# A gated linear attention followed by a routed expert layer: work reordered in the attention stage, tables turned, banks kept

## The chip, the cores and the metric

The kernel runs on one core of one Trainium2 chip. Times are device microseconds (us) of that core, from one launch. Engines are called PE (matrix products, with PEld for its weight loads), DVE (vector), ACT (scalar), POOL (GpSimd) and SP (which only issues transfers here). Each engine executes its own instructions strictly in the order in which the program issues them.

## The reference

q, k, v and alpha have shape (4 batches, 8 heads, 768 rows, 48). Per batch and head a 48x48 state is kept:

```
state = alpha[t][:, None] * state + outer(k[t], v[t])
y[t]  = q[t] @ state
x     = y with the heads side by side, (3072, 384)
on    = x @ w_skip > 0                     # rows that are computed at all
e     = argmax(x @ w_gate)  (8 experts)    # gate = softmax value of e
out   = x + gate * (relu(x @ w1[e]) @ w2[e])   for rows that are on, else x
```

w1[e] is 384x1024 and w2[e] 1024x384. All is float32.

## The kernel before, in words

**Attention stage.** The 3072 rows are cut into 24 tiles of 128 rows, six per batch, the four batches in turn. Tile i arrives in one buffer `qkv` (alpha, k, q transposed, then v). DVE makes two scans along the rows, `suffix` (L212) and `prefix` (L222), whose results scale k and q (L228 and L232, nearly all on POOL). Step i of the loop in `attention` then issues on PE, in this order: `scores(i+1)` (L252, k times q), `inter(i)` (L289, the product of the old state with q, from tile 4 on), `turn_k(i+1)` (L273, up to tile 19), `rows(i-1)` (L336, the finished output turned back to rows, with the nine routing columns), `outer(i)` (L301, the state's update, up to tile 19) and `intra(i)` (L309, masked scores times v). `inter(i)` and `intra(i)` add into one accumulator `ps_y`, which ACT copies out in `take_y` (`xt`, L316); the next tile's `inter` writes the same tile of PSUM. ACT also copies scores (L258), keys (L275) and rows (L347); POOL masks the left half of the scores (L262), DVE the right half (L266) and updates the state (L328).

**Routing.** `route_group` handles tiles 0-7, 8-14 and 15-19 as groups, in small DVE instructions that the loop lets out a few per step (`tick`). It computes the chosen expert, the gate and the rank of each row within its expert; then for each tile a 128x256 one-hot matrix of the rank (`one_hot`; ACT in two instructions, L460 and L461, or DVE in one, L457), and `marks` (L470) multiplies it with the row numbers and gates to fill a table, slot by expert. The one-hot is the stationary operand, 128x128 twice. Tiles 20-23 go one by one through `route_one`. For expert 0 its rows from these late tiles are not fetched from memory but selected by a product with a one-hot (`late_rows`, L533), the others are fetched by an indirect transfer (`fetch_rows`, L560) and turned (`early_turn`); `first_turn` copies the sum out.

**Weights.** Every weight piece is split in a high and a low part: ACT casts (L589), DVE or POOL subtracts (L590). Expert 0's w1 and w2 are both split during attention, in 12 pieces of 512 columns on ACT and POOL; expert e+1's during expert e, w1 beside the `up` products and w2 beside the `down` products.

**Expert stage.** For each of 8 experts `up` issues 72 products (L648) in four groups g of 18, `turn` (L628) prepares the next expert's rows, `down` issues 48 products for each half (L663), and rows are scattered to memory (L668). Within expert 0, `finish_table` adds the last marks after `up(0, 0)`. The attention's PSUM pool is closed before, and new ones (`ps_x`, `ps_h`, `ps_o`, `ps_f`) are opened.

## Time and profile before

| | us |
|---|---|
| median of 3 runs | 301.01 |
| lowest and highest | 300.92, 301.5 |
| the profiled execution | 301.59 |
| its span, first to last instruction | 299.9 |

| engine | busy us | share of the span | instructions |
|---|---|---|---|
| PE | 278.0 | 93% | 2831 |
| DVE | 201.4 | 67% | 393 |
| ACT | 142.9 | 48% | 290 |
| POOL | 152.1 | 51% | 176 |

A share is a mean over stages with different limits. PE counts as busy at either clock: the granted TensorE clock is 1.00 at its full level (2.4 GHz) and 0.50 at the lower one (1.2 GHz), and its mean over this execution is 0.939.

### The profile page before, as it was taken

The numbers are of one execution on the slowest core, as the hardware profiler recorded it, in microseconds if no ns is written. First come the engines' busy times: TensorE is split into PE (matmuls) and PEld (weight loads), VectorE is DVE, ScalarE is ACT, GpSimd is POOL, SyncE is SP. The second block draws the span as 40 slices with busy tenths as digits, with TensorE's granted clock in tenths as the row PEclk, the third lists the DMA queues.
The fourth block names the chain that finished last, engine by engine and source line by source line (L and its number), as shares of the span: only waits on it lengthen the run. The fifth ranks groups of instructions, "written<-read, shape, count | busy, mean of one in ns | idle before, by whom it ended". The sixth has DMA issues, their size and how long they took to land.

```text
span 299.9 us, 7149 instructions
## 1 busy us (share of the span) xinstructions
PE 278.0 (93%) x2831; PEld 260.0 (87%) x2831; DVE 201.4 (67%) x393; ACT 142.9 (48%) x290; POOL 152.1 (51%) x176
## 2 busy tenths in 40 slices
PE   7799999998998899779499999999999999999991
PEld 7689888887887787668499999999999999999990
DVE  5889788986778667743637675776757686785410
ACT  4335544668855954332328165471726538173200
POOL 6579987798779887551127431505133150302111
PEclk9789999999799989756979999999999999999998
DMA  7998899898489964342004676564667645550000
GB/s 240 320 375 300 283 313 313 275 318 294 155 271 322 316 228 138 105 115 105 26 3 108 251 256 237 184 211 163 228 234 249 233 165 178 198 208 26 12 29 20
DMA packets 20201, 60.04 MB, mean 200 GB/s; under 512 B 3272, under 2 KB 7181, under 8 KB 20160
## 3 DMA queue, kind: packets, MB, share of 16 engines
q1 hardware_dynamic: 17984, 54.43, 53.5%
q0 software_dynamic: 2176, 5.08, 4.8%
q8 instruction: 24, 0.39, 0.5%
q14 instruction: 17, 0.14, 0.1%
HBM read 52.46 MB, written 8.65 MB: 204 GB/s over the span
## 4 chain that ended last, share of the span: by engine, by line
PE 82%; DVE 9%; ACT 4%; POOL 2%; issue 1%; DMA 1%; POOLq 0%; DVEq 0%
PE ps_h L648 23%; PE ps_o L663 22%; PE ps_s L252 8%; PE ps_y L309 6%; PE ps_g L336 6%; PE ps_y L289 4%; PE ps_v L301 3%; PE ps_k L273 3%; PE ps_v L470 2%; DVE sfx L212 2%; PE ps_x L628 2%; DVE pfx L222 2%; ACT far L460 1%; PE ps_k L336 1%; DMA qkv<-in_tiles_dram 1%
## 5 line engine op out<-in xcount | busy, mean ns | idle before, releaser
L668 POOL DMA_INDIRECT out_dram<-o,idx x16 | 22.5, 1408 | 92.2 <-DVE o L666 92.2
L648 PE MATMUL ps_h<-xx,w1h 128*128 128x256 f32 x384 | 59.6, 286 | 3.1 <-DVE all L457 3.1
L648 PEld LDWEIGHTS ps_h<-xx,w1h 128*128 128x128 f32 x384 | 52.6, 193 | 3.4 <-ACT idg L434 3.3
L652 ACT ACTIVATE hh<-ps_h 128x512 fp32r<-128x512 f32 x32 | 19.1, 598 | 70.5 <-PE ps_h L648 69.8
L663 PE MATMUL ps_o<-w2h,hh 128*128 128x384 f32 x128 | 43.6, 341 | 0.0
L663 PE MATMUL ps_o<-w2h,hl 128*128 128x384 f32 x128 | 43.0, 336 | 0.0
L663 PE MATMUL ps_o<-w2l,hh 128*128 128x384 f32 x128 | 43.0, 336 | 0.0
L653 DVE SCALAR_TENSOR_TENSOR hl<-ps_h,hh 128x512 fp32r<-128x512 f32 x32 | 22.1, 692 | 20.8 <-ACT hh L652 20.5
L648 PE MATMUL ps_h<-xx,w1l 128*128 128x256 f32 x192 | 34.4, 285 | 0.0
L228 POOL TENSOR_TENSOR qkv<-qkv,sfx 112x512 f32<-112x512 f32 x24 | 28.5, 1187 | 11.5 <-DVE sfx L212 9.2
L252 PE MATMUL ps_s<-qkv 48*128 48x128 f32 x384 | 30.6, 300 | 3.0 <-DVE qkv L232 2.8
L252 PEld LDWEIGHTS ps_s<-qkv 48*128 48x128 f32 x384 | 25.8, 201 | 8.0 <-issue 5.5
L212 DVE TENSOR_TENSOR_SCAN sfx<-qkv,ps_d 112x524 f32<-112x524 f32 x24 | 29.6, 1233 | 3.8 <-DMA qkv<-in_tiles_dram 3.8
L309 PE MATMUL ps_y<-st,qkv 128*48 128x128 f32 x384 | 31.8, 306 | 0.0
L666 DVE SCALAR_TENSOR_TENSOR o<-ps_o,gates,xr 128x384 f32<-128x384 f32 x16 | 9.9, 618 | 31.0 <-PE ps_o L663 31.0
L222 DVE TENSOR_TENSOR_SCAN pfx<-qkv,ps_d 112x524 f32<-112x524 f32 x24 | 29.6, 1235 | 0.2
L560 POOL DMA_INDIRECT xr<-out_dram,idx x18 | 22.0, 1225 | 13.4 <-DVE gates L618 5.6
L648 PEld LDWEIGHTS ps_h<-xx,w1l 128*128 128x128 f32 x192 | 28.2, 193 | 0.0
L232 POOL TENSOR_TENSOR qkv<-qkv,pfx 112x512 f32<-112x512 f32 x22 | 26.2, 1190 | 3.4 <-DVE pfx L222 3.3
L590 DVE TENSOR_TENSOR w1l<-raw,w1h 128x768 fp32r<-128x768 f32 x28 | 26.9, 960 | 0.8
L589 ACT CAST w1h<-raw 128x768 fp32r<-128x768 f32 (+1 forms) x34 | 26.8, 789 | 0.0
L309 PEld LDWEIGHTS ps_y<-st,qkv 128*48 128x48 f32 x384 | 24.9, 138 | 0.6 <-issue 0.4
(166 smaller groups left out, 518.9 us busy)
## 6 DMA issues: line engine op xcount, KB each, us to landing
raw<-in_w_dram SPq DMA_DIRECT2D x64, 384.0 KB, 4.8
qkv<-in_tiles_dram SPq DMA_DIRECT2D x21, 966.0 KB, 6.7
out_dram<-x SPq DMA_DIRECT2D x24, 192.0 KB, 6.0
qkv<-in_tiles_dram SPq DMA_DIRECT2D x3, 262.0 KB, 5.1
out_dram<-xr SPq DMA_DIRECT2D x4, 192.0 KB, 7.6
qkv<-in_tiles_dram SPq DMA_DIRECT2D x1, 704.0 KB, 4.3
qkv<-in_tiles_dram SPq DMA_DIRECT2D x2, 256.0 KB, 3.5
qkv<-in_tiles_dram SPq DMA_DIRECT2D x1, 512.0 KB, 5.4
```

The costliest lines, as they stand in the source:

```text
L212: nc.vector.tensor_tensor_scan(sfx[:PD][:, ::-1], w["alpha"][:PD][:, ::-1], self.c_r[:PD].to_broadcast([PD, AW]), LOW, ALU.mult, ALU.max)
L222: nc.vector.tensor_tensor_scan(pfx[:PD], w["alpha"][:PD], self.c_f[:PD].to_broadcast([PD, AW]), 0.0, ALU.mult, ALU.max)
L228: (eng or self.nc.gpsimd).tensor_tensor(w["kh"][:PD], w["kh"][:PD], w["sfx"][:PD, :, 3:SEG], ALU.mult)
L232: (eng or nc.gpsimd).tensor_tensor(w["qh"][:PD], w["qh"][:PD], w["pfx"][:PD, :, 2:2 + P], ALU.mult)
L252: nc.tensor.matmul(self.ps_s[h][:, p * P:(p + 1) * P], lhsT=kh[r, p, :], rhs=qh[r, p, :], start=True, stop=True)
L309: nc.tensor.matmul(self.y_out(i, p, h), lhsT=w["v"][:, o:o + D], rhs=w["st"][:, h, p * P:(p + 1) * P], start=(i < B and p < 2), stop=(p >= 2))
L589: nc.scalar.copy(out=hi[:, s], in_=raw[:, s])
L590: (nc.gpsimd if early else nc.vector).tensor_tensor(lo[:, s], raw[:, s], hi[:, s].bitcast(F32), ALU.subtract)
L648: nc.tensor.matmul(ps[:, u, :], lhsT=a[:, k, f * P:(f + 1) * P], rhs=xx[:, k, b, :], start=(n == 0), stop=(n == len(order) - 1))
L653: nc.vector.scalar_tensor_tensor(out=hl, in0=ps, scalar=0.0, in1=hh.bitcast(F32), op0=ALU.max, op1=ALU.subtract)
L663: nc.tensor.matmul(ps, lhsT=a[:, f, js], rhs=b[:, f, :], start=(n == 0), stop=(n == 3 * FT - 1))
L668: ins = nc.gpsimd.indirect_dma_start(out=self.out[:, :], out_offset=bass.IndirectOffsetOnAxis(ap=self.idx[:, e, j:j + 1], axis=0), in_=o, ...
```

## The change

- **Order.** In a step, `inter(i)` is issued after `rows(i-1)`, before `outer(i)`. For tile 0 `outer`, `intra` and `carry` stand before `scores(1)`.
- **Start.** Loads are cut and ordered anew; the first tile's scans go in halves, with products by halves on DVE and POOL. The zero fills of `xw`, `stb`, `xtb` move from POOL to DVE, those of the three row buffers to ACT (one per step 1 to 3), and `route_constants` from step 3 to the start. For tiles 0 and 1 the right half of the scores goes through ACT and POOL as the left does. There are 14 warm-up products, and 4 more behind `turn_k(0)`.
- **Routing.** Groups are tiles 0-5, 6-10, 11-15, 16-19, and 20 with 21; only 22 and 23 go alone. Ranks move from PSUM tile `ps_v` to `ps_g`. One-hots on ACT are let out two instructions at a time at fixed places of the step, before `rows` and, from step 15, at its end. The last group's four one-hots are made two on POOL and two on DVE. The small "+1e-9" moves to POOL.
- **Table.** `marks` takes the values (128x24) as the stationary operand and the one-hot as the moving one, one product of 256 columns per tile; the table is 24 by 256, and two small products turn it where indices are needed.
- **Late tiles.** `route_one` is regrouped, with the one-hot for expert 0 read straight from the rank's PSUM tile; the tail after the loop is reordered.
- **PSUM.** The attention's banks stay open; `up` uses `ps_k`, `ps_s0`, `ps_s1` in turn, `down` uses `ps_g` and `ps_v`, `turn` uses `ps_y`, tables `ps_d`.
- **Weights.** Only w1 of expert 0 is split during attention (8 pieces of 384 columns, cast and subtraction in alternate steps). w2 has one buffer for all experts and is split beside the same expert's `up` products; w1 of e+1 beside the `down` products of e. `turn(e+1)` stands between the two `down` halves.

```diff
@@ attention loop, step i
-            advance(fetch, 2 if i >= 19 else 1 if i % 2 == 0 else 0)
+            if i in FETCH:
+                advance(fetch, FETCH[i])
...
-            if i == 9:
-                split = self.split_pieces(0, early=True)
-            if i + 1 < NT:
+            if i == 6:
+                split = self.split_pieces(0, "w1", 384)
+            ready, self.mark_jobs = self.mark_jobs[:1], self.mark_jobs[1:]
+            if i == 0:
+                self.outer(0)
+                self.intra(0)
+                self.take_y(0)
+            if not last:
                 self.scores(i + 1)
...
-            self.inter(i)
...
+            advance(self.hots, 2)
+            if 1 <= i <= 3:
+                self.clear_rows(i - 1)
...
+            self.flush(self.rank_jobs)
+            self.add_groups()
             if i > 0:
                 self.rows(i - 1)
...
-            self.tick(2 if i < 15 else 4 if i < LATE else 8)
...
-            self.outer(i)
-            self.intra(i)
-            self.carry(i)
-            self.take_y(i)
+            self.tick(3 if i < 15 else 4 if i < LATE - 1 else 5 if last else 8)
+            if last:
+                solo = self.route_one(i - 1)
+                advance(solo)
+            if i > 0:
+                self.inter(i)
+                self.outer(i)
+                self.flush(ready)
+                self.flush(self.soon)
+                self.intra(i)
+                self.carry(i)
+                self.take_y(i)
@@ marks
-        for j in range(NB):
-            for k, hot in enumerate(hots):
-                nc.tensor.matmul(ps[:, j, :], lhsT=hot[:, j * P:(j + 1) * P], rhs=V[k],
-                                 start=(j == 0 and k == 0), stop=(j == NB - 1 and k == len(hots) - 1))
+        for k, hot in enumerate(hots):
+            self.nc.tensor.matmul(ps, lhsT=V[:, k, :], rhs=hot, start=(k == 0), stop=(k == len(hots) - 1))
@@ route_group
-        yield nc.vector.tensor_scalar(out=s1, in0=s1, scalar1=1e-9, scalar2=None, op0=ALU.add)
+        nc.gpsimd.tensor_scalar(out=s1, in0=s1, scalar1=1e-9, scalar2=None, op0=ALU.add)
...
+                hots[k] = self.one_hot(r1[:, k, :], nc.gpsimd if k < n // 2 else nc.vector)
@@ split_pieces, experts
-        pool = self.wpool[e % 2]
+        pool = self.wpool["w2" if name == "w2" else e % 2]
...
+            second = self.split_pieces(e, "w2")
             for g in range(FT // 2):
+                if e > 0 or g > 1:
+                    advance(second)
                 self.up(e, g)
-                if (e, g) == (0, 0):
-                    self.finish_table()
-                advance(split)
+                if (e, g) == (0, 1):
+                    advance(second)
+            advance(second)
...
+            advance(first, 2)
+            self.down(e, 0)
             if e + 1 < E:
                 self.turn(e + 1)
+            advance(first, 2)
+            self.down(e, 1)
@@ up, down
-        ps = self.ps_h.tile([P, 2, CAP], F32, name="ps_h")
+        ps = (self.ps_k, *self.ps_s)[self.up_bank % 3].rearrange("p (u s) -> p u s", u=2)
-        ps = self.ps_o.tile([P, DM], F32, name="ps_o")
+        ps = (self.ps_g, self.ps_v)[j][:, :DM]
@@ the tail after the loop
+        for k in range(KT):
+            self.late_rows(LATE, k)
         self.rows(b)
+        advance(solo)
+        for k in range(KT):
+            self.late_rows(LATE + 1, k)
...
+        last = self.route_one(b)
+        advance(last)
         self.late_split(b)
...
         for j in range(NB):
             self.early_turn(j)
...
         for k in range(KT):
             self.late_rows(b, k)
+        advance(solo)
+        advance(last)
         self.first_turn()
```

## Rows read from the trace of the kernel before

**Rows 1.** Windows by stage: us from start, engine busy us (instructions), clock, DMA share, GB/s.

```profile
0.00:10.69 10.69, 7.00 (x52) 6.57 (x53) 7.01 (x11) 4.38 (x10) 7.14 (x16) 1.00 0.73 231
10.69:33.98 23.29, 23.08 (x309) 20.25 (x309) 20.21 (x33) 10.24 (x24) 18.53 (x27) 0.85 0.94 341
33.98:106.04 72.06, 69.21 (x1105) 60.28 (x1106) 56.87 (x119) 47.55 (x112) 61.50 (x71) 0.98 0.87 288
106.04:150.17 44.13, 35.65 (x360) 30.62 (x359) 26.25 (x103) 15.52 (x44) 22.38 (x32) 0.77 0.35 112
150.17:154.24 4.07, 4.07 (x22) 4.07 (x22) 0.00 (x0) 0.30 (x1) 0.23 (x1) 0.58 0.01 2
154.24:293.30 139.06, 139.01 (x988) 138.19 (x987) 90.47 (x130) 64.92 (x102) 41.33 (x31) 1.00 0.49 171
```

**Rows 2.** Chain that ended last, one step of the middle: start us, length us, what.

```profile
38.61 1.09 PE ps_s L252 x16
39.71 0.58 PE ps_y L289 x16
40.29 0.53 PE ps_k L273 x4
40.82 0.89 PE ps_g L336 x8
41.71 0.54 PE ps_v L301 x13
42.25 0.93 PE ps_y L309 x16
```

**Rows 3.** The same chain at the start of the kernel.

```profile
3.59 1.26 DVE sfx L212
...
10.69 2.51 PE ps_s L252 x16
```

**Rows 4.** DVE groups by line, 33.98 to 106.04: busy us, mean ns | idle before.

```profile
L222 DVE TENSOR_TENSOR_SCAN pfx<-qkv,ps_d 112x524 f32<-112x524 f32 x15 | 18.5, 1235 | 0.0
L212 DVE TENSOR_TENSOR_SCAN sfx<-qkv,ps_d 112x524 f32<-112x524 f32 x14 | 17.2, 1231 | 0.0
L266 DVE COPY_PREDICATED st<-mask,ps_s 128x512 f32<-128x512 uint8 x14 | 10.3, 732 | 4.2 <-PE ps_s L252 4.2
L328 DVE TENSOR_TENSOR state<-ps_v,old 112x192 f32<-112x192 f32 x14 | 4.8, 346 | 0.3 <-PE ps_v L301 0.3
L341 DVE TENSOR_REDUCE ps_d<-ps_g 128x9 f32<-128x36 f32 x14 | 2.7, 194 | 3.2 <-ACT x L347 3.0
```

**Rows 5.** Timeline at 72 us: start, length, engine, instruction [idle before <-releaser].

```profile
72.46 0.58 ACT L316 COPY xt<-ps_y 112x512 f32<-112x512 f32 x1
...
73.09 0.66 PE L289 MATMUL ps_y<-qkv,old 48*48 48x128 f32 x16 [1.09 <-ACT xt L316]
```

**Rows 6.** Timeline at 118 us, one POOL and one DVE instruction.

```profile
118.28 1.27 POOL L590 TENSOR_TENSOR w2l<-raw,w2h 128x512 fp32r<-128x512 f32 x1 [0.63 <-ACT w2h L589]
...
118.51 1.06 DVE L406 TENSOR_SCALAR s<-s 128x5 f32<-128x5 f32 x1
```

**Rows 7.** Timeline at 122 us, the last group's one-hots and marks.

```profile
122.35 2.04 DVE L457 TENSOR_SCALAR hot<-ps_d,r 128x256 fp32r<-128x256 f32 x5
...
122.97 2.93 PE L470 MATMUL ps_v<-V,hot 128*128 128x24 f32 x10 [1.35 <-DVE hot L457]
```

**Rows 8.** Timeline at 148 us: last part of expert 0's rows, first product.

```profile
147.83 0.41 DVE L556 TENSOR_TENSOR xx<-ps_v,xx 128x256 fp32r<-128x256 f32 x1
...
150.17 0.36 PE L648 MATMUL ps_h<-xx,w1h 128*128 128x256 f32 x1 [3.14 <-DVE all L457]
```

**Rows 9.** Chain that ended last: four products of 256 columns at the full clock.

```profile
141.16 0.48 PE ps_s L533 x4
```

**Rows 10.** Groups by line and form over the whole run, expert stage.

```profile
L590 DVE TENSOR_TENSOR w2l<-raw,w2h 128x768 fp32r<-128x768 f32 x28 | 25.5, 951 | 0.0
...
L653 DVE SCALAR_TENSOR_TENSOR hl<-ps_h,hh 128x512 fp32r<-128x512 f32 x32 | 22.1, 692 | 20.8 <-ACT hh L652 20.5 <-issue 0.4
```

More of the change, by code (lines that the diff above doesn't have):

```diff
@@ L107, in pools @@
         self.ps_d = bank.tile([P, 4 * P], F32, name="ps_d")
-        self.qkv = [fix.tile([P, TW], F32, name=f"qkv{i}") for i in range(NQ)]
         self.stb = [fix.tile([P, 2, NP * P], F32, name=f"st{i}") for i in range(2)]
@@ L426, in route_group @@
-        if g1 == LATE:
-            idx = self.indices(0, 1, "idx0")
-            self.fetch_rows(self.xr0, idx[:, 0, :])
-            self.work["early"] = True
+        if g0 >= LATE:
+            for k in range(n):
+                self.work[g0 + k]["mark"] = self.one_hot(r1[:, k, :], nc.vector, g0 + k)
+                yield
+            return
+        if g1 == LATE:
+            hots = [None] * n
+            for k in range(n):
+                hots[k] = self.one_hot(r1[:, k, :], nc.gpsimd if k < n // 2 else nc.vector)
+            self.rank_jobs.append(lambda: self.group_marks(g1, hots, V))
+            yield
@@ new lines, in route_group, with act_hots @@
+        yield nc.vector.tensor_reduce(out=add, in_=m.rearrange("p n e -> p e n"), op=ALU.add, axis=AX.X)
+        nc.gpsimd.tensor_tensor(self.cnt, add, self.cnt, ALU.add)
+        if g1 < LATE:
+            self.hots = chain(self.hots, self.act_hots(g1, r1, V, [None] * n, n))
+    def act_hots(self, g1, r1, V, hots, n):
+        nc = self.nc
+        for k in range(n):
+            far = self.sm.tile([P, CAP], F32, name="far")
+            nc.scalar.activation(out=far, in_=self.slots, func=AF.Abs, scale=-1.0, bias=r1[:, k, :])
+            yield
+            hots[k] = self.sm.tile([P, CAP], F32R, name="hot", bufs=8)
+            nc.scalar.activation(out=hots[k], in_=far, func=AF.Relu, scale=-1.0, bias=1.0)
+            if k == n - 1:
+                self.mark_jobs.append(lambda: self.group_marks(g1, hots, V))
+            yield
@@ new lines, in group_marks, with add_groups, early_rows @@
+    def group_marks(self, g1, hots, V):
+        ps = self.ps_v[:VW, 256:256 + CAP]
+        self.marks(ps, hots, V)
+        self.adds.append((g1, ps))
+    def add_groups(self):
+        for g1, ps in self.adds:
+            self.add_marks(ps)
+            if g1 == LATE:
+                self.soon.append(self.early_rows)
+        self.adds = []
+    def early_rows(self):
+        idx = self.indices(self.table(self.ps_v[:, 192:192 + NB * VW]), 0, 1, "idx0")
+        self.fetch_rows(self.xr0, idx[:, 0, :])
+        self.early = True
@@ L431, in gates, with first_hot @@
+    def first_hot(self, i, r1):
+        hot0 = self.work[i]["hot0"] = self.late.tile([P, CAP], F32R, name=f"hot{i}")
+        self.nc.vector.tensor_scalar(out=hot0, in0=self.iota, scalar1=r1, scalar2=self.m0[:, i - LATE:i - LATE + 1],
+                                     op0=ALU.is_equal, op1=ALU.mult)
     def gates(self, g0, g1, gate):
@@ L503, in route_one @@
-        pr = w["pg"][:, 424:424 + E]
-        def ranks():
-            nc.tensor.matmul(pr, lhsT=self.tri, rhs=m, start=True, stop=False)
-            nc.tensor.matmul(pr, lhsT=self.one_b, rhs=self.cnt, start=False, stop=True)
-        yield from self.defer(ranks)
-        t0 = t1("t0")
-        nc.vector.tensor_tensor(t0, pr[:, 0:1], m[:, 0:1], ALU.mult)
-        w["hot0"] = hot0 = self.late.tile([P, CAP], F32R, name=f"hot{i}")
-        yield nc.vector.tensor_scalar(out=hot0, in0=self.iota, scalar1=t0, scalar2=None, op0=ALU.is_equal)
@@ L577, in split_pieces @@
[L577 to L591 removed]
+        src = dict(w1=self.w1, w2=self.w2)[name]
@@ L609, in finish_table, with finish_rows @@
     def finish_table(self):
-        ps = self.ps_f.tile([P, 2 * 3 * E], F32, name="ps_f")
-        self.marks(ps, *self.last_marks)
+        ps = self.ps_d[:VW, 0:CAP]
+        self.marks(ps, [self.work[i]["mark"] for i in range(LATE, NT)], self.late_vals)
         self.add_marks(ps)
-        self.idx = self.indices(0, E, "idx")
+    def finish_rows(self):
+        tab = self.table(self.ps_d[:, CAP:CAP + NB * VW])
+        self.idx = self.indices(tab, 0, E, "idx")
         for n in (1, 0):
@@ L907, in attention @@
         self.scale_k(2)
-        ends = {g[1]: g for g in GROUPS}
-        solo = {}
+    def attention(self):
+        nc, advance = self.nc, self.advance
+        self.start()
+        fetch = chain(self.weight_pieces(0, "w1"), self.weight_pieces(0, "w2"), self.weight_pieces(1, "w1"))
+        split = iter(())
+        groups = {g[1]: g for g in GROUPS + ((LATE, LATE + 2),)}
         for i in range(NT):
+            last = i + 1 == NT
             if i + NQ - 1 < NT:
```

436 lines of the change are left out of this document (231 added, 205 removed).

## The prediction, made before the change was run

> **What bounds the kernel now.** I read the windows by stage first, then the chain that ended last, then single places of the timeline. In the windows [rows 1] the reader should look at PE's busy time beside the length, and at the clock. From 154.24 to 293.30, the expert stage, PE is busy for 139.01 of 139.06 us at the full clock: nothing but fewer products can shorten it. The attention stage is another matter. From 33.98 to 106.04 (14 steps, from `scores(6)` to `scores(20)`) PE is busy 69.21 of 72.06 us at a mean clock of 0.98. From 106.04 to 150.17 it is busy only 35.65 of 44.13 us, at 0.77; since the clock has two levels, 1.00 and 0.50, a mean of 0.77 says that 2 x 0.23 x 44.13 = 20.3 us passed at the lower one. The first products of expert 0 (150.17 to 154.24) ran at 0.58. So the loss sits in the last five steps, the hand-over to the experts, and a little before them.
>
> The chain gives the price of a full step at the full clock [rows 2]: 1.09 + 0.58 + 0.53 + 0.89 + 0.54 + 0.93 = 4.56 us, PE without a gap. DVE's groups over the same 14 steps [rows 4] sum to 18.5 + 17.2 + 10.3 + 4.8 + 2.7 = 53.5 us, 3.8 a step (all its work there is 56.87 [rows 1]). DVE is therefore the next limit, 15% below PE.
>
> **Sums are made against the profiled execution**, 301.59 us (span 299.9 and 1.7 around it); the median of the runs shown is 301.01, 0.6 lower, and I take off 0.6 at the end.
>
> **A, start up to `scores(6)` at 33.98.** Before, `scores(1)` begins at 10.69 and takes 2.51 us [rows 3] where the same 16 products take 1.09 later [rows 2]: PE had idled and its clock had fallen. In 10.69 to 33.98 the clock is 0.85 [rows 1], so 2 x 0.15 x 23.29 = 7.0 us at half, which costs 3.5 us; idle time is only 0.2 us. The change puts tile 0's update and output products and four warm-ups into the wait before `scores(1)`, and moves POOL's fills away. But DVE cannot follow without end: it is busy 20.21 of these 23.29 us, so only 3.1 us can go before DVE is the limit, 0.9 more if one counts that two right-half masks (0.73 each [rows 4]) leave it and that some half products and second scans (some 0.6) come to it. Before that, the first scan stands at 3.59 [rows 3], behind the transfer of alpha; the large fills now run on DVE in the time that it waits there. Bounds: no gain, even 0.5 us lost, if the fills are late or a new gap drops the clock again; 4.0 us gained. I take the middle, 2.0, because PE still has to wait for masked scores of tile 0 and for tile 2's scaling, either of which can cost a fall of the clock.
>
> **B, steps 5 to 18, 33.98 to 106.04.** 14 x 4.56 = 63.8 us is PE's work at the full clock. To it come marks: 16 one-hots at one product of 256 columns each, 0.12 by [rows 9], 1.9 us (before: two stationary one-hots a tile, so nothing is added); ranks, three groups of at most 7 small products, some 0.3 each, 0.9. That makes 66.6. What is to go: at 73.09 `inter` had waited 1.09 us for ACT's `xt`, which ended 0.05 us earlier [rows 5], because ACT had one-hots and casts to do first; `inter` had only `scores` (1.09 us) as cover. In the new order PE first meets `xt` at `rows`, behind `turn_k` as well, 0.53 us later [rows 2], and ACT's one-hots are let out two instructions at a time and not directly before `xt`. ACT also loses w2's casts. What is late next is DVE: 14 steps of 3.8 us plus some 3 us of small routing work for each of three groups is 53.5 + 9 = 62.5, close to 66.6, and it comes in bursts. I add 1.3 us for such bursts: 67.9 us, a gain of 4.2. Bounds: 0 (waits move) to 5.5 (72.06 - 66.6).
>
> **C, from `scores(20)` to the first product of expert 0, 44.13 us.** PE's work at the full clock: step 19 without `turn_k`, 1.09 + 0.89 + 0.58 + 0.54 + 0.93 = 4.0; steps 20 to 22 without `outer` too, 3.5 each, 10.5; step 23 without `scores`, 2.4; the last `rows` 0.9; 24 late products and 12 turns at 0.12 [rows 9], 4.3; marks, ranks and the table's two turns, some 2.2. Together 24.3.
>
> Waits. The last group's marks: before, five one-hots on DVE took 2.04 us in a row and PE stood 1.35 us [rows 7]; now four are shared by two engines and come a step later, I keep 0.9. `rows(22)` has no `scores` before it, so `xt(22)` is open: 0.58 [rows 5] and its handing over, 0.7. The last tile's ranks, one-hot and the first copy of the sum: 1.4, nearest the 0.41 to 0.58 that one such instruction takes [rows 5, 8]. Together 3.0.
>
> The hand-over itself: expert 0's rows were ready at 147.83 + 0.41 = 148.24, and the first product began at 150.17 after 3.14 us of idling, behind one-hots and gates that it does not read [rows 8]. With the banks kept open I expect the first product behind the first copy; 1.9 us goes, and the low parts, read last in this group, are no longer waited for.
>
> The clock: before, about 20 us at half. The waits above are each under 1.1 us, but several stand close together; I keep one fall, 5 us at half, which costs 2.5. Sum 24.3 + 3.0 + 2.5 = 29.8, taken as 30.0: a gain of 14.1. Bounds: 25.0 if no clock falls, 38 if the clock stays as low as before (10.1 us lost instead of 2.5).
>
> The early fetch for expert 0 moves a step later and is queued on POOL behind the store of tile 20; `early_turn` waits for it. It is issued some 9 us before, and needs it last in the tail, so I cost it at nothing; without that cover it is 1 to 2 us, inside the bounds.
>
> **D, first products of expert 0.** 18 products and 4 marks at 0.12 [rows 9] are 2.6 us against 4.07 at clock 0.58 [rows 1]. I take 1.3 gained, with bounds of 0 and 1.5.
>
> **E, expert stage.** The number of products is unchanged. w2 is now split beside `up`, in one buffer that the previous `down` must have read. One `up` phase is 72 products, 8.6 us; DVE does four subtractions of 0.951 and four low parts of 0.692 in it [rows 10], 6.6 us, and an output combination. The last quarter of w2 is read three quarters into the first `down`. So it costs nothing. If that cover fails, four subtractions and a cast stand open, 4.7 us an expert. Expert 0's w2, until now split in attention, fits the same phase.
>
> **The sum.** 301.6 - 2.0 - 4.2 - 14.1 - 1.3 = 280.0, and 0.6 less against the median: 279.4 us.
>
> **A rule that speaks against it.** At 118.51 a DVE instruction on five columns took 1.06 us; it ended at 119.57, as the POOL subtraction beside it did (118.28 + 1.27) [rows 6]. The Trainium skill, "SBUF — State Buffer", section "SBUF: two separate sides", says that VectorE and GpSimd share a pair of SBUF ports which one of them holds for a whole instruction while the other is blocked. The trace agrees. By that rule the change's new half products on DVE and its one-hots on POOL take turns with the other engine, and A would come to nothing.
>
> **The rivals.**
> 1. *The late stage stays a chain at half the clock.* For: about 20 us at half now, and ranks, one-hots and copies remain in sequence. Against: the pair (20, 21) and the regrouped `route_one` take most DVE work out of the tail. C then gives 6 and D nothing, B 3, A 2: 301.6 - 11.0 - 0.6 = 290.0 us.
> 2. *The wait moves and does not go.* `rows(i-1)` reads the same `xt(i-1)` that `inter(i)` waited for, with only 0.53 us more cover against a wait of 1.09 [rows 2, 5]; one fall of the clock in the middle stays. B gives 1.5: 282.1 us. That would mean that the reordering does not do what it says.
> 3. *DVE and POOL block one another* as at 118.5 [rows 6]. A gives nothing: 281.4 us. This is the result by the page's rule.
> 4. *Slower: w2's single buffer.* If the split cannot run beside `up` (late transfer, or a buffer held until `down` ends), each expert waits up to 4.7 us: 8 x 4.7 = 37.6 against 22 gained, 317 us. It decides from 2.7 us an expert. For: DVE is at 6.6 of 8.6 us there, plus the output. Against: PE is never held by DVE's lag before the first `down`, and pieces are read in the order in which they are made.
>
> **How the numbers follow.** Forecast 56%, rival 1 22%, rival 2 10%, rival 3 8%, rival 4 4%. The likeliest case's own range is 275 to 284 (C between 25 and 33, A and B by 1 to 2 each way). The range for all reaches up to rival 1, 291, and down to 274, which needs almost every bound at its best; outside are rival 4, the worse half of rival 1 and a little below. A measurement can tell about 0.2% from no change. Faster by more than that holds in all cases but rival 4: 0.95; same 0.01; slower 0.04.
>
> **What would show it.** In the new profile: `scores(1)` at about 1.1 us and not 2.5, and `scores(6)` near 32 (A); no wait of `inter` or `rows` for `xt` above 0.5 us in the middle, and steps near 4.6 (B); first product of expert 0 near 127 to 131 with less than 1 us of idling before it (C); first group in about 2.6 us (D); 17.6 us for each later expert, PE without gaps (E). It would be wrong if the clock stands at 0.50 for more than 10 us between `scores(20)` and the experts, or if PE idles before any `down`.

## The result, and the profile after

The changed kernel took 284.03 us in the median of four runs, the kernel before 300.97 beside it; the ratio is 0.9402, 95% interval 0.9309 to 0.9495. One of the four runs, 424.65 us at a mean clock of 0.559, was disturbed; medians here and below are of all runs, while a ratio leaves such longer runs out. The other three are 280.51, 283.38 and 284.69. The profiled execution is the one of 280.51 us (span 278.7), the shortest of the four, so the sum, made for a profiled execution, is to be held against it: 280.0 forecast, 280.51 found.

The windows by stage of the changed kernel, cut at 10.69 us and then at the same events as [rows 1] (`scores(6)`, `scores(20)`, expert 0's first product, its second group, the end of the last `down`); the columns are those of [rows 1]:

```profile
0.00:10.69 10.69, 9.22 (x72) 8.65 (x72) 8.81 (x18) 4.61 (x10) 6.05 (x18) 1.00 0.80 261
10.69:31.84 21.15, 19.71 (x292) 17.08 (x293) 20.06 (x34) 12.66 (x28) 18.99 (x23) 1.00 0.97 358
31.84:98.27 66.43, 66.43 (x1096) 57.47 (x1095) 57.71 (x126) 43.10 (x107) 55.73 (x74) 1.00 0.92 306
98.27:129.66 31.39, 27.94 (x351) 23.91 (x349) 22.58 (x78) 15.94 (x44) 23.67 (x39) 0.95 0.37 123
129.66:132.53 2.87, 2.87 (x24) 2.81 (x25) 1.46 (x4) 0.61 (x2) 0.23 (x1) 1.00 0.00 0
132.53:272.13 139.60, 139.52 (x990) 138.31 (x989) 96.30 (x133) 69.92 (x106) 36.10 (x31) 1.00 0.53 182
```

The reader is to see that the clock is 1.00 everywhere but in the fourth stretch, and that PE has no gap in the third and the last. The differences to [rows 1], stretch by stage:

| stage | before us | after us | difference | forecast |
|---|---|---|---|---|
| start to `scores(6)` (A) | 33.98 | 31.84 | -2.14 | -2.0 |
| to `scores(20)` (B) | 72.06 | 66.43 | -5.63 | -4.2 |
| to expert 0's first product (C) | 44.13 | 31.39 | -12.74 | -14.1 |
| its first group (D) | 4.07 | 2.87 | -1.20 | -1.3 |
| the rest of the experts (E) | 139.06 | 139.60 | +0.54 | 0 |

They sum to -21.17, and the spans differ by 21.2 (299.9 to 278.7).

**Start.** PE's timeline; the first line answers to the second of [rows 3]:

```profile
12.45 1.16 PE L271 MATMUL ps_s<-qkv 48*128 48x128 f32 x16
...
15.11 1.16 PE L271 MATMUL ps_s<-qkv 48*128 48x128 f32 x16 [0.96 <-DVE qkv L251]
```

`scores(1)` starts 1.8 us later than before but runs in 1.16 us instead of 2.51; `scores(2)` waits 0.96 us for DVE's scaled q. From 10.69 us to `scores(6)` PE's work shrank from 23.08 to 19.71 us and its idle time grew from 0.21 to 1.44; the difference is the gain.

**Middle.** One step of the chain of waits, against [rows 2]: start, length, what.

```profile
31.91 1.09 PE ps_s L271 x16
33.00 0.53 PE ps_k L292 x4
33.54 0.89 PE ps_g L359 x8
34.42 0.58 PE ps_y L312 x16
35.01 0.54 PE ps_v L324 x13
35.54 0.93 PE ps_y L332 x16
```

The same six pieces at the same lengths, 4.56 us, in the new order. The wait of [rows 5] is gone; from `scores(6)` to `scores(20)` PE's timeline has no wait of 0.3 us or more. DVE's costliest groups there are unchanged against [rows 4]:

```profile
L240 DVE TENSOR_TENSOR_SCAN pfx<-qkv,ps_d 112x524 f32<-112x524 f32 x15 | 18.5, 1235 | 0.2
L227 DVE TENSOR_TENSOR_SCAN sfx<-qkv,ps_d 112x524 f32<-112x524 f32 x14 | 17.2, 1229 | 0.0
L285 DVE COPY_PREDICATED st<-mask,ps_s 128x512 f32<-128x512 uint8 x14 | 10.2, 730 | 2.8 <-PE ps_s L271 2.6
```

**Late.** The one-hots of the group of tiles 16 to 19 (against [rows 7]), two on DVE and two on POOL, and the marks that read them:

```profile
110.30 0.88 DVE L525 TENSOR_SCALAR hot<-ps_d,r 128x256 fp32r<-128x256 f32 x2
...
111.65 1.84 POOL L525 TENSOR_SCALAR hot<-slots,r 128x256 fp32r<-128x256 f32 x2
...
112.64 0.30 PE L531 MATMUL ps_v<-hot,vals 128*24 128x256 f32 x1 [0.54 <-POOL hot L525]
...
113.54 0.53 PE L531 MATMUL ps_v<-hot,vals 128*24 128x256 f32 x3 [0.60 <-POOL hot L525]
```

Eight microseconds on, a small addition from the routing of the pair (tiles 20 and 21), a POOL subtraction, and the first selection:

```profile
120.26 1.23 DVE L438 TENSOR_TENSOR cnt<-add,cnt 128x8 bf16<-128x8 f32 x1
120.46 1.00 POOL L607 TENSOR_TENSOR latel<-x,lateh 128x384 fp32r<-128x384 f32 x1
...
122.00 0.42 PE L593 MATMUL ps_s<-hot,lateh 128*128 128x256 f32 x1 [1.49 <-DVE hot L496]
```

The addition is over eight columns and takes 1.23 us; it begins 0.20 us before the POOL instruction beside it and ends with it (121.49 and 121.46). PE stands 1.49 us. Behind that wait its clock falls, by the windows of the next three stretches:

```profile
122.00:123.00 1.00, 1.00 (x5) 1.00 (x6) 0.93 (x6) 0.00 (x0) 0.20 (x2) 0.60 0.00 0
123.00:125.00 2.00, 2.00 (x12) 1.97 (x11) 0.78 (x4) 0.50 (x3) 1.61 (x4) 0.50 0.77 163
125.00:126.00 1.00, 1.00 (x9) 1.00 (x7) 0.67 (x2) 0.54 (x2) 0.00 (x0) 0.69 0.95 372
```

The hand-over, which had 3.14 us of idling [rows 8], has 0.29:

```profile
129.66 0.39 PE L710 MATMUL ps_k<-xx,w1h 128*128 128x256 f32 x1 [0.29 <-ACT xx L614]
```

### The profile page after: what moved, and what is told of

Read it like the earlier page. It is cut to its first block, busy times and chain, and to the rows that moved or that the text cites. A ratio compares the mean times of both kernels' runs of the same rounds, so it can differ in the third digit from the quotient of the medians.

```text
span 278.7 us, 7136 instructions
## 1 busy us (share of the span) xinstructions
PE 265.7 (95%) x2819; PEld 248.2 (89%) x2819; DVE 207.5 (74%) x390; ACT 146.8 (53%) x295; POOL 141.8 (51%) x184
## 4 chain that ended last, share of the span: by engine, by line
PE 84%; DMA 5%; DVE 5%; POOL 1%; SPq 1%; issue 1%; ACT 1%; POOLq 0%; DVEq 0%
PE ps_s L710 16%; PE ps_g L729 12%; PE ps_v L729 12%; PE ps_k L710 9%; PE ps_s L271 7%; PE ps_y L332 6%; PE ps_g L359 6%; DMA qkv<-in_tiles_dram 5%; PE ps_y L312 4%; PE ps_v L324 4%; PE ps_k L292 3%; PE ps_y L690 2%; PE ps_k L359 1%; SPq L219 1%; PE ps_v L531 1%
## 5 line engine op out<-in xcount | busy, mean ns | idle before, releaser
L710 PE MATMUL ps_s<-xx,w1h 128*128 128x256 f32 x252 | 39.5, 283 | 0.0
L710 PEld LDWEIGHTS ps_s<-xx,w1h 128*128 128x128 f32 x252 | 34.4, 191 | 0.1
L650 DVE TENSOR_TENSOR w2l<-raw,w2h 128x768 fp32r<-128x768 f32 x32 | 30.8, 965 | 2.2 <-ACT w2h L647 1.5
L247 POOL TENSOR_TENSOR qkv<-qkv,sfx 112x512 f32<-112x512 f32 (+1 forms) x25 | 28.6, 1144 | 7.5 <-DVE qkv L231 3.8
L647 ACT CAST w2h<-raw 128x768 fp32r<-128x768 f32 x32 | 26.4, 829 | 7.2 <-issue 7.2
L240 DVE TENSOR_TENSOR_SCAN pfx<-qkv,ps_d 112x524 f32<-112x524 f32 (+1 forms) x25 | 29.8, 1193 | 0.5
L227 DVE TENSOR_TENSOR_SCAN sfx<-qkv,ps_d 112x524 f32<-112x524 f32 (+1 forms) x25 | 29.5, 1185 | 0.5 <-DMA qkv<-in_tiles_dram 0.5
L251 POOL TENSOR_TENSOR qkv<-qkv,pfx 112x512 f32<-112x512 f32 (+1 forms) x23 | 26.9, 1170 | 5.3 <-DVE pfx L240 4.9
L332 PE MATMUL ps_y<-st,qkv 128*48 128x128 f32 x384 | 27.3, 275 | 0.5 <-POOL st L281 0.5
L339 ACT COPY xt<-ps_y 112x512 f32<-112x512 f32 x24 | 14.1, 586 | 24.3 <-PE ps_y L332 24.3
L359 PE MATMUL ps_g<-xw,xt 112*128 112x105 f32 x176 | 23.7, 277 | 0.5 <-ACT xt L339 0.5
L729 PE MATMUL ps_v<-w2h,hh 128*128 128x384 f32 x64 | 22.0, 344 | 0.0
```

The lines of the kernel that those rows point to most:

```text
L227: nc.vector.tensor_tensor_scan(sfx[:PD, a:a + n][:, ::-1], w["alpha"][:PD, a:a + n][:, ::-1], self.c_r[:PD].to_broadcast([PD, n]), LOW, AL ...
L240: nc.vector.tensor_tensor_scan(pfx[:PD, a:a + n], w["alpha"][:PD, a:a + n], self.c_f[:PD].to_broadcast([PD, n]), 0.0, ALU.mult, ALU.max)
L247: (eng or self.nc.gpsimd).tensor_tensor(w["kh"][:PD, s], w["kh"][:PD, s], w["sfx"][:PD, s, 3:SEG], ALU.mult)
L251: (eng or nc.gpsimd).tensor_tensor(w["qh"][:PD, s], w["qh"][:PD, s], w["pfx"][:PD, s, 2:2 + P], ALU.mult)
L332: nc.tensor.matmul(self.y_out(i, p, h), lhsT=w["v"][:, o:o + D], rhs=w["st"][:, h, p * P:(p + 1) * P], start=(i < B and p < 2), stop=(p >= 2))
L359: nc.tensor.matmul(pg[:, p, :], lhsT=w["xt"][:PD, p, :], rhs=self.xw[:PD, p, :], start=True, stop=True)
```

## The experiments

Kernels of one group ran on one chip, each with the kernel before beside it (medians 300.97, 300.77, 300.52 and 301.10). "Late stretch" is the time from `scores(20)` to expert 0's first product.

### The changed kernel again

> The changed kernel once more, nothing edited. Three of its executions took 280.51, 284.69 and 283.38 us, the profiled one being the fastest, while four of the kernel before lie between 299.97 and 301.5. Theory 1: the late stage holds or loses the clock by small shifts, so another execution differs from the profiled one between scores(20) and the first product of expert 0 (31.3 us there), by 1.5 to 4 us, and nowhere else. Theory 2: the start is bound by transfers (the chain has 14 us of transfers of tiles before 18 us), so another execution differs before scores(6), which stood at 31.91, by 1 to 3 us. Median expected 282 to 284, ratio to the kernel before 0.94.

Measured: 280.96 us (278.58 to 284.61, 6 runs), ratio 0.9316 (0.9252 to 0.9379). The runs fall into two groups, 278.58 to 278.99 at mean clocks of 0.994 to 0.997 and 282.93 to 284.61 at 0.976 to 0.983. Its profiled execution (278.58) has the clock at 1.00 through the late stretch:

```profile
97.99:128.09 30.10, 26.42 (x351) 22.36 (x349) 22.58 (x78) 15.95 (x44) 23.68 (x39) 1.00 0.40 127
```

PE waits in the same places for the same lengths (0.52, 0.61, 0.52, 1.50); the clock did not fall behind the last, and the stretch is 1.3 us shorter than in the execution above. So 30.10 us, 26.42 of them PE at work, is the stretch without a fall. `scores(6)` starts at 31.57, 0.27 us earlier. Both executions are among the shorter ones, so neither theory on the longer runs is settled here; the start of such runs is looked at further down.

### `inter` back ahead of `turn_k` and `rows`

```diff
@@ changed kernel, step i, behind scores(i+1) and take_scores(i+1)
+            if i > 0:
+                self.inter(i)
...
             if i > 0:
-                self.inter(i)
                 self.outer(i)
```

> The changed kernel with the old-state product put back in front of turn_k and rows, all else kept. Theory 1 (the cover of the new order is what ended the waits in the middle): inter again waits for xt behind ACT's one-hots and casts, steps with one-hots lose 0.5 to 1 us, the stretch from scores(6) to scores(20) grows from 66.4 to 69 to 71 us, the median by 2.5 to 5 us. Theory 2 (the one-hots' new places on ACT did it, not the order): ACT has nothing before xt in most steps, the stretch stays below 67.5 us and the median within 1 us.

Measured: 279.37 us (278.42 to 281.43), ratio 0.9299 (0.9258 to 0.9341). Middle stage of its trace:

```profile
31.40:97.83 66.43, 66.43 (x1095) 57.48 (x1094) 57.25 (x126) 44.28 (x107) 55.71 (x74) 1.00 0.93 304
```

66.43 us without a gap, as with the new order. In the changed kernel the order is not what ends the waits; theory 1 fails. That it is the places of the one-hots, as theory 2 has it, is not shown by this run alone, for w2's casts have left ACT as well.

### The kernel before with `inter` moved, and nothing else

```diff
@@ kernel before, step i
-            self.inter(i)
...
             advance(split)
+            self.inter(i)
             self.outer(i)
```

> The kernel before with one edit: the old-state product is issued behind rows, before outer. Theory 1 (cover): the waits of 0.65 to 1.09 us between 72 and 108 us go, the stretch from scores(6) to scores(20), 72.06 us, falls to 68 to 69.5 us, the median by 2.5 to 4 us. Theory 2 (places of the one-hots): ACT still reaches xt late, rows now waits for it with 0.53 us more cover, the stretch stays above 70.5 us and the median within 1.5 us of 301.

Measured: 295.68 us (291.68 to 298.35), ratio 0.9773 (0.9716 to 0.983): 5.3 us less than before. The middle of its trace in three windows, and PE's timeline inside the third:

```profile
33.91:52.20 18.29, 18.29 (x306) 15.92 (x306) 15.26 (x31) 8.63 (x20) 15.61 (x19) 1.00 0.90 292
52.20:95.70 43.50, 43.50 (x718) 38.17 (x717) 37.51 (x82) 31.31 (x77) 39.93 (x47) 1.00 0.91 294
95.70:104.88 9.18, 8.31 (x86) 7.08 (x84) 5.05 (x8) 7.35 (x18) 7.03 (x8) 0.70 0.97 344
```

```profile
97.86 0.28 PE L470 MATMUL ps_v<-V,hot 128*128 128x24 f32 x1 [0.30 <-ACT hot L461]
98.71 0.73 PE L470 MATMUL ps_v<-V,hot 128*128 128x24 f32 x5 [0.57 <-ACT hot L461]
```

From 52.20 to 95.70 PE has no gap, where it stood 1.88 us before (43.50 long, 41.62 busy, clock 0.96). So the order alone does end the waits for `xt`. What remains are two waits for ACT's one-hots, 0.30 and 0.57 us, behind which one step takes 9.18 us at a clock of 0.70; the changed kernel, with its one-hots at fixed places, has neither. With that one step, the whole stretch to `scores(20)` takes 70.97 us in this execution, only 1.1 us less than before: by its length theory 2, though the waits for `xt` went as theory 1 has it. Another 5.1 us were gained in the late stretch (39.07, clock 0.85 instead of 0.77), for which no run here shows the cause. Taken with the last experiment: the order alone ends the waits for `xt`, and so does the rest of the change without it; only the rest also ends the waits for one-hots. Their gains do not add.

### PSUM banks closed and opened again

```diff
@@ changed kernel: the pool of ps_s, ps_y, ps_k, ps_g, ps_v, ps_d is closed
@@ behind attention, and one of the same shapes is opened for the experts
+            self.banks(st)
```

> The changed kernel with its PSUM pool closed after the attention stage and an identical one opened for the experts; same banks and order. Theory 1 (the closing is what the first product of expert 0 waited for): it waits again for the last one-hot and gates, starts 1.2 to 2 us later than in the changed kernel (129.66 there), and perhaps at the lower clock, 1.5 us more; median 1 to 3.5 us up. Theory 2 (the late order alone brought the hand-over): the last one-hots are early enough, the first product starts within 0.4 us of the copies, median within 0.5 us.

Measured: 281.68 us (280.2 to 285.58), ratio 0.9341 (0.9301 to 0.9381). The one-hot that the first product does not read, and the first product:

```profile
131.93 0.47 DVE L529 TENSOR_SCALAR all<-ps_d,r 128x256 fp32r<-128x256 f32 x1
...
132.55 0.36 PE L715 MATMUL ps_k<-xx,w1h 128*128 128x256 f32 x1 [1.90 <-DVE all L529]
```

The old wait is back, 1.90 us, and the late stretch is 31.70 at clock 1.00 against 30.10: keeping the banks is worth 1.6 us there. Behind the wait expert 0's first group takes 3.74 us at clock 0.68, against 2.87 at 1.00, 0.9 us more. The medians (281.68, 280.96) alone would not show it.

### The pair's counts read from PSUM; the one-hots of tiles 16 to 19 all on DVE; both

```diff
@@ counts from PSUM: route_group, tiles 20 and 21
+            add = self.ps_d[:, 224:224 + E]
@@ one-hots on DVE: route_group, tiles 16 to 19
-                hots[k] = self.one_hot(r1[:, k, :], nc.gpsimd if k < n // 2 else nc.vector)
+                hots[k] = self.one_hot(r1[:, k, :], nc.vector)
```

> One part put back: in the last group's routing the running counts (add) are read from PSUM again, as in the kernel before, where this addition of 128x8 took 0.17 us; in the changed kernel its operand is in SBUF, and it took 1.23 us beside GpSimd's copy of 1.00 us (latel). Theory 1 (that DVE instruction is held while GpSimd works in SBUF, and the chain to the last one-hots is late by it): the addition takes about 0.2 us, the PE wait of 1.49 us ahead of the last marks falls to about 0.5, the clock behind it stays up, the stretch scores(20) to first product of expert 0 falls from 30.1 to 31.3 us to 28 to 29, and the time falls by 1 to 2.5 us against the repeat of the changed kernel (280.96), to 278.5 to 280. Rival 2 (the hold moves on to the next DVE instruction with SBUF operands, or another chain is just behind): the addition is short, the PE wait stays over 1.2 us, time within 0.6 us. Rival 3 (an operand in PSUM makes DVE and ScalarE or PE meet there): slower by 0.3 us or more.

> The one-hots of the last group all on DVE, instead of two on GpSimd, where they took 1.84 us together against 0.88 us for the two on DVE. Theory 1 (PE waits 0.54 and 0.60 us for GpSimd's one-hots): these two waits go, the last group's marks end about 1 us earlier, but the 1.49 us wait for the last one-hots behind them is set by DVE's chain and GpSimd's copy; the stretch from scores(20) to the first product falls by 0.5 to 1.1 us. Rival 2 (DVE is the engine that sets the last chain; 0.9 us more on it comes back one for one): the two waits go and the last wait grows from 1.49 to 2.0 to 2.4 us, time unchanged within 0.5 us, or slower by up to 1 us if the clock falls longer behind it.

> Both edits: counts read from PSUM in the last group, and its one-hots all on DVE. Theory 1 of both (the late stretch of 30.1 to 31.3 us holds waits of 0.54, 0.60 and 1.49 us and a stretch of halved clock behind the last): the stretch falls to 27.5 to 28.5 us, time about 278 us against 280.96 for the repeat, most of it from the clock. If the two only shift the wait along the same DVE chain: 30 us and no change beyond 0.6 us.

| | late stretch | PE's waits there | median (lowest, highest) | ratio |
|---|---|---|---|---|
| changed kernel again | 30.10 | .52 .61 .52 1.50 | 280.96 (278.58, 284.61) | 0.9316 |
| counts from PSUM | 29.03 | .54 .60 .52 .43 | 279.43 (277.65, 281.55) | 0.9286 (0.9233 to 0.9338) |
| one-hots on DVE | 29.22 | .44 .52 1.50 | 281.08 (277.75, 281.94) | 0.9339 (0.9288 to 0.9389) |
| both | 28.14 | .45 .52 .43 | 279.65 (278.57, 281.10) | 0.93 (0.9258 to 0.9342) |

The addition with one operand in PSUM, the POOL subtraction and the first selection, in the first of the three:

```profile
124.38 0.17 DVE L439 TENSOR_TENSOR cnt<-ps_d,cnt 128x8 bf16<-128x8 f32 x1
...
124.58 1.01 POOL L608 TENSOR_TENSOR latel<-x,lateh 128x384 fp32r<-128x384 f32 x1
...
125.05 0.38 PE L594 MATMUL ps_s<-hot,lateh 128*128 128x256 f32 x1 [0.43 <-DVE hot L497]
```

0.17 us instead of 1.23, and the wait falls from 1.50 to 0.43; 1.07 us goes from the wait and 1.07 from the stretch. The one-hots on DVE take 0.88 us off the stretch: the two waits for POOL's one-hots become one of 0.44. The two edits add (1.96). In the stretch, theory 1 holds for each, and rival 2 of the second (DVE late by as much) fails: its last wait stays at 1.50. The medians do not show these gains cleanly, because the start differs from execution to execution; in the first and third of these profiled executions `scores(6)` came at 35.96 and 35.58, in the second at 31.55.

### The start: tile 0's products back behind `scores(1)`

```diff
@@ changed kernel, step 0
-            if i == 0:
-                self.outer(0)
-                self.intra(0)
-                self.take_y(0)
             if not last:
                 self.scores(i + 1)
...
-            if i == 0:
-                self.carry(0)
...
-            if i > 0:
+            if i >= 0:
                 self.inter(i)
                 self.outer(i)
```

> One move undone at the start: the first chunk's old-state product and its neighbours stand behind scores(1) again, as before. Theory 1 (in the changed kernel the work of chunk 0 fills the idle time ahead of scores(1), which so runs in 1.16 us at a granted clock of 1.00, where before it took 2.51 us after a fall): scores(1) takes over 2 us again, scores(6) starts at 33 to 34 us instead of 31.4 to 31.9, and the time grows by 1.5 to 2 us. Rival 2 (the start is set by the transfers and DVE, and the order of PE's work there is free): scores(6) within 0.5 us of 31.9, time unchanged.

Measured: 280.86 us (278.94 to 281.29), ratio 0.9322 (0.928 to 0.9365).

```profile
12.93 1.80 PE L271 MATMUL ps_s<-qkv 48*128 48x128 f32 x16 [2.88 <-ACT ends L255]
```

PE now idles 2.88 us, `scores(1)` takes 1.80 us, and `scores(6)` starts at 34.07, 2.2 us later than in the first profile of the changed kernel, as theory 1 expected. But the median is that of the repeat, and the two profiles differ in more than the edit: in this one a DVE product of the start was held for 2.08 us, in that one not (next section). Against the executions of the other kernels that were held in the same way (`scores(6)` at 34.42, 35.58 and 35.96) this start is no later. So what placing tile 0's products ahead of `scores(1)` is worth is not shown.

### Fillers at the start, alone and with both edits above

```diff
@@ changed kernel, step i; a call of fill is a 128x128 product of zeros into ps_g that nothing reads
+            if i < 2:
+                self.fill(5 if i == 0 else 8)
             if not last:
                 self.scores(i + 1)
```

> The changed kernel with products of zeros that nothing reads put on PE at the start: five (0.67 us) ahead of scores(1) and eight (1.07 us) ahead of scores(2), where PE stood 0.8 and 1.0 to 1.5 us. The executions of the changed kernel and of its variants so far lie near 278 to 279 or near 281 to 284.7; of the profiled ones, the longer had a stretch at 0.50 between 13 and 23 us (scores(6) at 34 to 36) and the shorter none (31.6). Theory 1 (what varies is whether the clock falls in these first waits, and idling of PE is what lets it): scores(6) at 31.5 to 32.5 in the profiled execution with no stretch at 0.50 before it, the spread of the executions shrinks to about 1 us, median 279 against 280.96. Rival 2 (the clock falls by something else, and the waits are its mark and not its cause): spread and median as before, within 0.6 us. Rival 3 (PE is on the path there): 0.5 to 1.5 us slower.

> The same fillers at the start together with both edits to the last group (counts read from PSUM, all four one-hots on DVE). If the start's clock fall and the late waits are separate and each is cured: scores(6) at 31.5 to 32.5, the stretch from scores(20) to the first product 28.1 us as with both edits alone, median 276.5 to 277.5 with a spread of about 1 us. If fillers do nothing: 279.65 as with both edits alone, within 0.6.

First the start of an execution without fillers in which the clock fell (the one with counts from PSUM): POOL's and DVE's halves of one product for tile 1, what POOL did behind its half, `scores(1)`, `scores(2)`, and the window behind the wait.

```profile
9.27 0.69 POOL L247 TENSOR_TENSOR qkv<-qkv,sfx 112x256 f32<-112x256 f32 x1 [0.94 <-DVE sfx L227]
9.31 2.10 DVE L247 TENSOR_TENSOR qkv<-qkv,sfx 112x256 f32<-112x256 f32 x1
...
9.91 1.23 POOL L281 TENSOR_SCALAR_AFFINE_SELECT st<-st 128x512 f32<-128x512 f32 x2
...
13.07 1.31 PE L271 MATMUL ps_s<-qkv 48*128 48x128 f32 x16 [0.82 <-DVE qkv L251]
...
16.46 2.08 PE L271 MATMUL ps_s<-qkv 48*128 48x128 f32 x16 [1.54 <-DVE qkv L251]
```

```profile
18.00:20.00 2.00, 2.00 (x14) 1.78 (x12) 2.00 (x3) 1.02 (x3) 1.82 (x2) 0.50 1.02 425
```

Behind waits of 0.82 and 1.54 us the granted clock stands at 0.50, the 1.2 GHz level, until about 22.5. The waits begin with DVE's half product, which took 2.10 us. In the repeat of the changed kernel DVE began first, and the same product took 0.42:

```profile
8.98 0.42 DVE L247 TENSOR_TENSOR qkv<-qkv,sfx 112x256 f32<-112x256 f32 x1
9.09 0.85 POOL L247 TENSOR_TENSOR qkv<-qkv,sfx 112x256 f32<-112x256 f32 x1 [1.20 <-DVE qkv L231]
```

The ten profiled executions of the changed kernel and its variants part in the same way. In five (the first, the repeat, `inter` moved back, one-hots on DVE, fillers with both edits) DVE began first, by 0.01 to 0.12 us, and its half took 0.40 to 0.42 us; the clock stayed at 1.00 in their starts. In the other five POOL began 0.04 or 0.05 us ahead, and DVE's half took 2.08 to 2.10 us; in the four of them without fillers the clock fell. This is what the traces show; no run changed the halves themselves, and what decides which engine begins first stays open. With fillers alone, in an execution in which DVE's half was held (2.09 us):

```profile
12.95 1.16 PE L277 MATMUL ps_s<-qkv 48*128 48x128 f32 x16
...
14.48 1.96 PE L214 MATMUL ps_g<-const-float32-0.0 128*128 128x128 f32 x16
16.37 1.16 PE L277 MATMUL ps_s<-qkv 48*128 48x128 f32 x16
```

Fillers alone: 280.12 us (279.71 to 280.84), ratio 0.9323 (0.9289 to 0.9356); `scores(6)` at 32.89, no stretch below 1.00 in the start, all six clocks at 0.992 or more. Fillers and both edits: 278.35 us (277.75 to 279.12), ratio 0.9256 (0.9222 to 0.9289); late stretch 28.14 again. The spread falls from 6.0 us to 1.1 and 1.4, as theory 1 expected, and in the profile the clock stays up behind the same held product: the fillers do not remove the late operand, they keep the clock from falling behind it. The unfilled kernel did not run on this chip; on the two chips where it and its variants ran six times each the spreads were 2.4 to 6.0 us. The fillers have a price: a call took 0.25 us (16 records, two a call, in 1.96 us), not the 0.13 that was counted, so PE was on the path. It shows in the profile with both edits, where nothing was held: `scores(1)` starts at 13.68 and `scores(6)` at 33.63, against 12.18 and 31.57 in the repeat. So in these profiles a start without a held product loses 2 us and a held one gains (32.89 against 34.42 to 35.96). The medians came about 1 us over the forecasts, and by ratio the fillers alone give a steady time and no shorter one (0.9323 against the repeat's 0.9316). The kernel with both has the lowest median and ratio of all, though its interval meets that of both edits alone; in its group its longest run (279.12) is under the shortest of the one with fillers alone (279.71).

### How much of the late gain is the clock: fillers in the kernel before

```diff
@@ kernel before; first try | second try (numbers of calls)
+            self.fill(i, {20: 5, 22: 4, 23: 12}.get(i, 0))   | {20: 2, 22: 2, 23: 9}
             self.inter(i)
...
+            self.fill(LATE + 2, 10)    # ahead of the last group's marks | 4
+        self.fill(NT, 7)               # ahead of the last tile's selection | 4
+        self.fill(NT, 22)              # ahead of expert 0's first product | 10
```

> The kernel before with products of zeros that nothing reads, some 0.13 us each, put into PE's waits of its late stage: 5, 4 and 12 ahead of inter(20), inter(22), inter(23), 10 ahead of the last group's marks, 7 ahead of the last tile's selection, 22 ahead of expert 0's first product; all else as before. In before about 20 us of the stretch from scores(20) to the first product pass at 0.50, a cost of about 10 us; the changed kernel has 12.8 us less there in all. Theory 1 (most of the late gain is the clock): the stretch falls from 44.1 to 36 to 38 us, its clock to over 0.93, the first group of up to 2.6 us, and the time by 6 to 9 us, to 292 to 295. Rival 2 (the chain of DVE, ACT and POOL behind the late tiles sets the end, and at the full clock PE only waits longer): the stretch stays over 41 us and the time falls by less than 3 us. Rival 3 (the fillers delay the work behind them): slower.

Measured: 304.53 us (303.77 to 305.24), ratio 1.0124 (1.0087 to 1.0161), late stretch 47.17. Slower by 1.2%, as rival 3 had it, and by a miscount: a call is two records and took 0.23 us, so the last 22 calls lasted 5.07 us in a wait of 3.14.

```profile
148.98 5.07 PE L202 MATMUL ps_y<-const-float32-0.0 128*128 128x128 f32 x44
```

> The kernel before with fewer fillers in the waits of its late stage: 2, 2 and 9 calls ahead of inter(20), inter(22), inter(23), 4 ahead of the last group's marks, 4 ahead of the last tile's selection, 10 ahead of expert 0's first product. A call took 0.23 us in the last try, twice what it was counted at, so the fillers there were longer than the waits (10.1 us for a wait of 3.14 and three others) and that time says little of the clock. The fillers ahead of inter(23) now write a bank that is free, so they no longer wait for xt. Theory 1 (most of the late gain of the changed kernel is the clock): scores(20) to first product falls from 44.1 to 36 to 38 us, time 292 to 295. Theory 2 (the chain over DVE, ACT and POOL sets the end: ACT's copy xt(22) stood behind a gate's cast that waits for DVE, and came at 133.81 in before and at 132.80, 0.06 us earlier counted from scores(20) with its 0.95 us shift, though the clock was up): the clock of the stretch is over 0.93 and yet it lasts 41 to 44 us, the first group of up takes 2.6 instead of 4.07, and the time falls by 1.5 to 4 us, to 296.5 to 299.

Measured: 299.27 us in the median of 12 runs (295.34 to 303.26), ratio 0.989 (0.984 to 0.994). The late stretch of its profiled execution, and the first product of expert 0:

```profile
109.51:147.86 38.35, 35.10 (x421) 30.85 (x421) 25.41 (x103) 14.55 (x42) 21.98 (x31) 1.00 0.38 123
```

```profile
147.86 0.35 PE L656 MATMUL ps_h<-xx,w1h 128*128 128x256 f32 x1 [0.91 <-DVE all L465]
```

The clock is at 1.00 throughout and the stretch is 38.35 us instead of 44.13. Theory 2 (41 to 44) fails; theory 1 is nearly met in the stretch (36 to 38) and missed in the time (292 to 295); this execution, of 298.56 us, lost 3.5 us ahead of `scores(20)`, where nothing was filled. The 0.06 us that theory 2 was given for is a slip: `xt(22)` came 27.77 us behind `scores(20)` before (133.81 - 106.04) and 25.81 in the first try (132.80 - 106.99), 1.96 earlier. Of the 35.10 us that PE is busy, the groups by line put 6.1 + 2.3 = 8.4 on fillers, so its own work is 26.7 us, against 26.42 in the changed kernel: at the full clock PE's work there has hardly changed. In the kernel before it was busy 35.65 us [rows 1], so half clock cost 35.65 - 26.7 = 8.9 us, and 44.13 - 35.65 = 8.5 us were idle. With the clock held up, 5.8 of the 8.9 are gained and 3.1 come back as waiting. The other 38.35 - 30.10 = 8.25 us of the late gain were not to be had by the clock in this execution: they go to the shorter chain over DVE, ACT and POOL and the hand-over. Of these the banks are 1.6; the other 6.6 us no run took apart. The split is an estimate from one execution, and fillers that outlast their wait would make the 8.25 too large.

## Why the prediction was right, step by step

**A (-2.0; found -2.14).** In the profiled execution the mechanism held: `scores(1)` at 1.16 us, `scores(6)` at 31.84, DVE busy 20.06 of 21.15 us and so next to the limit, as reckoned. But what I took as one number is one of two cases: over the profiled executions with the new start and no fillers `scores(6)` lay between 31.40 and 31.84 where DVE's half product ran freely, and between 34.42 and 35.96 where it was held behind POOL. In the second case A gains nothing and loses up to 2.0 us, more than the 0.5 that my bounds allowed. The doubt stated there, that a new wait can cost a fall of the clock, was right; that the wait comes from the change's own halves on DVE and POOL I left to rival 3. That the profiled execution met the forecast is in part luck: it was the shortest of its four.

**B (-4.2; found -5.63).** Right in sign, too small, with the reason only half right. PE's work was put at 66.6 us and is 66.43; the 1.3 us added for DVE's bursts was the error, there are none. DVE was reckoned at 62.5 us and is busy 57.71, so it was not close to PE. And the new order, to which I gave the first place, is not needed: with the rest of the change in place `inter` in the old place waits for nothing. Rival 2 (10%) fell: no wait of `inter` or `rows` moved into the middle.

**C (-14.1; found -12.74, or -14.03 in the repeat).** The sum came out close with its terms off in both directions, which is luck. PE's work was 26.4 us and not 24.3; the waits 3.7 us (30.10 - 26.42) and not 3.0; the clock 0 or 1.3 us and not 2.5. The lower bound, 25.0 without a fall of the clock, did not follow from the sum's own terms (24.3 + 3.0 = 27.3); without a fall the stretch took 30.10. Of the waits, 1.1 us stand at the marks of tiles 16 to 19 (put at 0.9), for POOL's one-hots, twice as dear there as on DVE, and 0.5 at `rows(22)` (put at 0.7). The largest, 1.5 us, stands where I put none, at the first selection, for the pair's one-hot behind the held addition; the last tile, put at 1.4, has waits of 0.3 us at most. The 1.9 of the hand-over (1.6 by the banks' experiment) was near. Rival 1 (22%, the stage stays at half clock) fell: the clock is 0.95 to 1.00. Its premise, that the late stage is a chain, was true of about half the loss, by the estimate above.

**D and E (-1.3 and 0; found -1.20 and +0.54).** The first group takes 2.87 us at clock 1.00. w2's single buffer costs nothing: PE is busy 139.52 of 139.60 us; where its 0.5 us more of work come from stays open. Rival 4 fell.

**Rival 3, DVE and POOL block one another.** I gave it 8%, and it came true in four of the eight profiled executions without fillers: in the start, at the half products that I named, whenever POOL began first. There the gain of A is gone (`scores(6)` at 34.07 to 35.96, 33.98 before). It also stands where I did not look, at one addition of eight columns, where it cost 1.07 us. The Trainium skill, "SBUF — State Buffer", section "SBUF: two separate sides", counts DVE operations with two SBUF inputs among those that need the shared ports. The traces agree: the half product with both operands in SBUF took 0.42 us when it began before POOL's and 2.10 when it began 0.04 us behind, to the end of POOL's next instructions and not of one alone; the addition took 1.23 us beside POOL with both operands in SBUF and 0.17 with one in PSUM. In both cases of the addition its record begins 0.20 us before POOL's, so there the order of the records does not tell which engine had to wait.

**Range and median.** The range, 274 to 291, holds 284.03 and the repeat's 280.96. The distance of the first median from 279.4 has no term in the sum. Its two longer runs (283.38 and 284.69) were not profiled; that their starts were held is likely from the profiled ones, of which those with a held start and no fillers took 280.74 to 284.47 and the others 277.75 to 280.51, but it is not shown.

## What to carry to other kernels

Ask of each wait of PE not only how long it is but what the clock does behind it: here a held product, the waits of 0.8 and 1.5 us behind it and the fall of the clock cost 4.4 us together (`scores(6)` at 35.96 and 31.57), and filling the waits with products that nothing reads made the time steady, though not shorter. When DVE and POOL share one product, look at several executions: here DVE's half ran freely where it began first, by 0.01 us or more, and was held where POOL was 0.04 us ahead. When several edits aim at one wait, test each alone on the old kernel and take each away from the new one; two that look additive may be substitutes. And price a late stage's loss in three parts, work at the full clock, half clock, idling: at the full clock some of the second turns into the third.

## What the hardware showed that I had not expected

- A 112x256 product on DVE with both operands in SBUF took 0.42 us when it began 0.11 us before POOL's half of the same work, and 2.10 us when POOL had begun 0.04 us before it; it ended 0.27 us behind POOL's third instruction from there.
- An addition of 128x8 on DVE took 1.23 us with both operands in SBUF while POOL subtracted 128x384 in SBUF; 0.17 us with one operand in PSUM.
- A 128x256 one-hot took 0.92 us on POOL (two in 1.84) and 0.44 on DVE (two in 0.88).
- A product of 128x128 zeros in float32 is two records and takes 0.23 to 0.25 us, not the 0.13 that its single record suggests.
- The clock's fall is not settled by the wait alone: behind the same wait of 1.49 to 1.50 us at 122 it fell to 0.50 in the first profile and stayed at 1.00 in the repeat.
